# Unit 0 of a gated recurrence with a feed-forward layer: sums of halves as identity matmuls, products unsplit, keys handled by thirds, and one weight tile loaded first

## The chip, the cores and the metric

One NeuronCore of a Trainium2 chip. The metric is device time in microseconds of one execution. Engines are named as in the profile: PE (TensorE matmul; PEld its weight loads), DVE (VectorE), ACT (ScalarE), POOL (GpSimd) and SP (SyncE, which issues most DMAs). Each engine works through its own queue strictly in the order fixed when the program is built; an instruction that has to wait holds up everything behind it on its engine.

## What is computed

```python
mag = sqrt(a_re*a_re + a_im*a_im)
scale = minimum(mag, 0.999) / (mag + 1e-06)          # the decay, kept below 1
a = (a_re + i a_im) * scale                          # per batch, head, time, key channel
for t in range(S):                                   # B, H, S, D = 4, 8, 768, 48
    state = a[t] * state + outer(k[t], v[t])         # complex state, 48 x 48 per head
    y[t]  = q[t] @ real(state)
x   = y, heads side by side                          # 3072 tokens x 384
out = ((x @ w_a) * (x @ w_b)) @ w_out                # d_ff 1536, all float32
```

## The kernel before

The sequence is cut into chunks of 128 steps. A **unit** is a pair of batches in one chunk: 12 units, six chunks for each pair. All eight heads of a unit lie as 384 rows of (head, channel), in three thirds j of 128 partitions, so a quantity of a unit is a tile of 128 partitions x 768 (three thirds x two batches x 128 steps).

A unit passes through these steps.

- `scale(u)` makes the decay factor from the squares of both parts, by Ln and Exp on ACT and one Newton step on DVE. For unit 0 it works in two halves of 384 columns, which load by two DMAs. The sum of the two squares is a DVE operation (L182).
- `prep(u)` multiplies the decays in (L214), then forms running products of them: seven steps within sub-blocks of eight (L230 multiplies, L236 adds; for unit 0 in two parts), a joining of the sub-blocks in small tiles, and then for the real and the imaginary part (k = 0, 1) two 768-wide products (L292) into `a_t` and their sum into `z` (L297). From z it makes the inverse: squares (L300), their sum (L306), Ln and Exp (L307, L308), one Newton step (L322, L324). Queries are multiplied with z (L312); keys with the inverse (L328) and then with z (L312).
- `stack(u)` copies queries and keys head by head into `stk` by ten DMAs from SP; for units 0 and 1 the queries go ahead of the keys.
- `attn(u)` is PE work with DVE and ACT between: scores (L385) and their masking (L388), outputs (L425) into `xh` and `xl`, transposes and the state.
- The feed-forward layer: for each of 12 blocks f of d_ff, `gemm1` (L486) and `gemm2` (L504). Each float32 factor is a pair of fast-format values, hi and lo.

The 36 weight tiles (12 blocks x 3 parts, 128 x 384) come as 64-bit words and are converted on the chip by `split_weights`. For each: three DVE operations (L137, L139, L141) assemble the values in a buffer `o_sb` (a pool of three, taken in turn), ACT rounds them to hi (L145), PE forms the value minus hi in PSUM with an identity and a negated identity (L150, L151), and ACT writes lo (L152). A buffer of o_sb is free again when L145 and L150 have read it. Here 18 tiles are written ahead of attention of unit 0 and 18 are spread over the feed-forward of unit 0, where `prep(1)` runs too. L675 in that stretch is a row of matmuls on the new keys of unit 1 ahead of its attention.

A build-time scheduler (the tile framework) sets the order of each engine's queue from the written order and the dependencies, so the conversions stand between the steps of unit 0, and some of the later 18 tiles too are ahead of its attention. SP issues the loads in the written order: decays of unit 0 in two halves, weight block 0, queries and keys, block 1, values, block 2, decays of unit 1, the other blocks.

Of the kernel before, what the change touches and what calls it, by code (L numbers as in the profile page):

```python
# [8 lines left out]
F32 = mybir.dt.float32  # L9
# [5 lines left out]
ALU = mybir.AluOpType  # L15
# [55 lines left out]
def tile_kernel(ctx: ExitStack, tc: tile.TileContext, a_d, qk_d, v_d, w_d, qn_d, kn_d, vn_d, an_d, out_d):  # L71
# [24 lines left out]
    biases = const.tile([128, 6], F32, name="biases")  # L96
    b_tiny, b_sq, b_eps, b_one, b_inv, b_rsq = (biases[:, i:i + 1] for i in range(6))
    vec.memset(b_tiny, TINY)
    vec.memset(b_sq, EPS * EPS * (1 + 2.0 ** -20))
    vec.memset(b_inv, LIFT * LN2)  # L100
# [24 lines left out]
    def load_weights(f):  # L125
        for m, (c0, n) in enumerate(WPART):
            raws[f, m] = wpool.tile([128, n, 2], U32, name=f"w{m}{f}")
            sync.dma_start(out=raws[f, m].rearrange("p c s -> p (c s)"),
                           in_=w_d[f, :, c0:c0 + n].bitcast(U32))

    def split_weights():
        for f in range(NF):
# [20 lines left out]
            yield  # L153
# [15 lines left out]

    def scale(u, a_t, tmp):  # L170
# [6 lines left out]
        for n, hs in enumerate(halves if u == 0 else (slice(0, W),)):  # L177
# [4 lines left out]
            vec.scalar_tensor_tensor(out=m, in0=m, scalar=-EPS * EPS, in1=x, op0=ALU.add, op1=ALU.add)  # L182
            act.activation(out=s0, in_=m, func=AF.Ln, bias=b_sq)
# [5 lines left out]
            vec.tensor_tensor(out=m, in0=m, in1=x, op=ALU.mult)  # L189
# [13 lines left out]
    def prep(u):  # L203
# [22 lines left out]
        parts = [(p * NB // 2, NB // 2) for p in range(2)] if u == 0 else [(0, NB)]  # L226
        for i in range(1, SUB):
            pr = small.tile([128, 2, 2, NB], F32, name="pr", bufs=1)
            for o, n in parts:
                vec.tensor_tensor(  # L230
                    out=pr[:, :, :, o:o + n],
                    in0=view(zz, W + at_(i) + 2 * o, [[W, 2], [-W, 2], [2, n]]),
                    in1=tok(slice(1, 3), i - 1, o, n).unsqueeze(1).broadcast_to([128, 2, 2, n]),
                    op=ALU.mult)
            for o, n in parts:
                vec.tensor_tensor(out=tok(slice(1, 3), i, o, n), in0=pr[:, :, 0, o:o + n],  # L236
                                  in1=pr[:, :, 1, o:o + n], op=ALU.add)
# [51 lines left out]
        for k in range(2):  # L289
            pz = a_t  # L290
            for s in range(2):
# [5 lines left out]
            vec.tensor_tensor(out=z[:, k].rearrange("p (b i e) -> p b i e", e=2, i=SUB // 2),  # L297
                              in0=view(pz[:], 0, PAIRS), in1=view(pz[:], W, PAIRS), op=ALU.add)
# [7 lines left out]
        vec.tensor_tensor(out=a_t[:, 0], in0=a_t[:, 0], in1=a_t[:, 1], op=ALU.add)  # L306
        act.activation(out=a_t[:, 1], in_=a_t[:, 0], func=AF.Ln, scale=2.0 ** LIFT, bias=b_tiny)  # L307
# [456 lines left out]
```

## Time and profile before

| | |
|---|---|
| median of 3 runs | 698.79 us (698.2 to 699.16) |
| the profiled execution | 698.89 us, span 697.2 us |
| busy: PE, PEld, DVE, ACT, POOL | 655.2, 610.8, 551.8, 308.9, 5.6 us |
| mean TensorE clock of the span | 0.974 of full speed |
| DMA | 63.94 MB, mean 92 GB/s; 300 to 400 GB/s in the first 45 us |

How to read its rows: a row of the timeline is start and duration in us, engine, line, operation, the tile written and those read, partitions x elements, and how many instructions are merged in it (x2); in square brackets stands the engine's idle time before it and what ended that. A float32 matmul shows as two records. Ends of matmuls are modelled. In a row of stretches each engine has its busy us and its number of instructions; then come the granted TensorE clock, the busy share of the DMA engines and GB/s.

### The profile page before, as it was taken

The numbers are of one execution on the slowest core, as the hardware profiler recorded it, in microseconds if no ns is written. First come the engines' busy times: TensorE is split into PE (matmuls) and PEld (weight loads), VectorE is DVE, ScalarE is ACT, GpSimd is POOL, SyncE is SP. The second block draws the span as 40 slices with busy tenths as digits, with TensorE's granted clock in tenths as the row PEclk, the third lists the DMA queues.
The fourth block names the chain that finished last, engine by engine and source line by source line (L and its number), as shares of the span: only waits on it lengthen the run. The fifth ranks groups of instructions, "written<-read, shape, count | busy, mean of one in ns | idle before, by whom it ended". The sixth has DMA issues, their size and how long they took to land.

```text
span 697.2 us, 14316 instructions
## 1 busy us (share of the span) xinstructions
PE 655.2 (94%) x5854; PEld 610.8 (88%) x5854; DVE 551.8 (79%) x1241; ACT 308.9 (44%) x618; POOL 5.6 (1%) x11
## 2 busy tenths in 40 slices
PE   3557999999999999999999999999999999999996
PEld 1224889899899999999999999999999999999996
DVE  5999899988888889989899898999989853232221
ACT  6357755634535445245363554535542332221221
POOL 3000000000000000000000000000000000000000
PEclk9567999999999999999999999999999999999999
DMA  8973202411414205134151340511510500400000
GB/s 312 402 291 108 79 1 54 129 55 55 128 42 130 81 28 149 60 98 129 25 160 46 102 134 1 169 67 47 145 46 2 165 25 17 106 24 2 24 1 28
DMA packets 32088, 63.94 MB, mean 92 GB/s; under 512 B 3984, under 2 KB 10640, under 8 KB 32016
## 3 DMA queue, kind: packets, MB, share of 16 engines
q1 hardware_dynamic: 28560, 58.23, 27.0%
q10 hardware_dynamic: 3456, 4.72, 1.9%
q8 instruction: 48, 0.79, 0.5%
q14 instruction: 24, 0.20, 0.1%
HBM read 39.32 MB, written 4.72 MB: 63 GB/s over the span
## 4 chain that ended last, share of the span: by engine, by line
PE 64%; DVE 27%; ACT 4%; DMA 2%; issue 1%; SPq 1%; ACTq 0%; DVEq 0%
PE ab L486 30%; PE o L504 14%; PE xp L425 6%; PE pm L385 5%; PE pm L442 4%; DVE a_t L292 3%; DVE pr L230 2%; DVE qk L312 2%; DVE h_t L495 2%; PE pm L396 2%; DVE hl L497 2%; PE pm L150 2%; DVE z L297 2%; DVE pb L260 1%; DVE z L236 1%
## 5 line engine op out<-in xcount | busy, mean ns | idle before, releaser
L486 PE MATMUL ab<-xh,w 128*128 128x256 f32 x1728 | 339.0, 285 | 0.0
L486 PEld LDWEIGHTS ab<-xh,w 128*128 128x128 f32 x1728 | 278.1, 190 | 1.8 <-issue 1.4
L486 PE MATMUL ab<-xl,w 128*128 128x256 f32 x864 | 245.1, 284 | 0.0
L486 PEld LDWEIGHTS ab<-xl,w 128*128 128x128 f32 x864 | 164.4, 190 | 0.5 <-issue 0.2
L504 PE MATMUL o<-w,hh 128*128 128x384 f32 x576 | 152.3, 344 | 0.0
L494 ACT COPY h_t<-ab 128x256 f32<-128x256 f32 x144 | 53.1, 369 | 176.9 <-PE ab L486 176.8
L495 DVE TENSOR_TENSOR h_t<-ab,h_t 128x256 f32<-128x256 f32 x144 | 60.5, 420 | 72.5 <-ACT h_t L494 72.3
L504 PEld LDWEIGHTS o<-w,hh 128*128 128x128 f32 x576 | 96.8, 190 | 3.7 <-issue 3.0
L504 PE MATMUL o<-w,hl 128*128 128x384 f32 x288 | 96.9, 336 | 0.0
L496 ACT CAST hh<-h_t 128x256 fp32r<-128x256 f32 x144 | 58.0, 403 | 81.1 <-DVE h_t L495 80.9
L497 DVE TENSOR_TENSOR hl<-h_t,hh 128x256 fp32r<-128x256 f32 x144 | 60.5, 420 | 17.5 <-ACT hh L496 17.3
L150 PE MATMUL ab<-o_sb,ident 128*128 128x384 f32 x42 | 29.1, 794 | 29.9 <-DVE o_sb L141 29.8
L385 PE MATMUL pm<-stk 128*128 128x128 f32 x384 | 54.4, 279 | 2.7 <-DMA stk<-qk 2.7
L504 PEld LDWEIGHTS o<-w,hl 128*128 128x128 f32 x288 | 54.1, 188 | 0.0
L385 PEld LDWEIGHTS pm<-stk 128*128 128x128 f32 x384 | 48.7, 191 | 5.9 <-issue 4.8
L230 DVE TENSOR_TENSOR pr<-z 128x384 f32<-128x384 f32 (+1 forms) x91 | 47.1, 524 | 2.4 <-ACT z L216 0.8
L150 PEld LDWEIGHTS ab<-o_sb,ident 128*128 128x128 f32 x42 | 10.2, 286 | 39.8 <-DVE o_sb L141 29.4
L292 DVE TENSOR_TENSOR a_t<-z,b_t 128x768 f32<-128x768 f32 x48 | 44.6, 952 | 0.1
L425 PE MATMUL xp<-am,v_t 128*32 128x128 f32 x768 | 42.5, 277 | 1.3 <-DVE am L388 1.2
L312 DVE TENSOR_TENSOR qk<-qk,z 128x1536 f32<-128x1536 f32 (+1 forms) x28 | 42.7, 1524 | 0.1
L388 DVE TENSOR_TENSOR am<-pm,mask 128x512 f32<-128x512 f32 x48 | 32.8, 685 | 5.0 <-PE pm L385 4.8
L425 PE MATMUL xp<-stk,u 128*32 128x128 f32 x640 | 34.4, 273 | 0.0
(106 smaller groups left out, 761.7 us busy)
## 6 DMA issues: line engine op xcount, KB each, us to landing
w<-in_dram SPq DMA_DIRECT2D x36, 384.0 KB, 8.1
qk<-in_dram SPq DMA_DIRECT2D x12, 768.0 KB, 4.8
a_t<-in_dram SPq DMA_DIRECT2D x11, 768.0 KB, 4.3
stk<-qk SPq DMA_DIRECT2D x42, 192.0 KB, 3.3
v_t<-in_dram SPq DMA_DIRECT2D x24, 256.0 KB, 2.7
out_dram<-o_sb ACTq DMA_DIRECT2D x24, 192.0 KB, 1.9
stk<-qk SPq DMA_DIRECT2D x18, 192.8 KB, 3.4
stk<-qk SPq DMA_DIRECT2D x14, 128.0 KB, 3.1
```

Of the source, the lines that this page charges most:

```text
L150: pe.matmul(out=lp[:, 0:n], lhsT=ident, rhs=t, start=True, stop=False)
L230: vec.tensor_tensor(out=pr[:, :, :, o:o + n], in0=view(zz, W + at_(i) + 2 * o, [[W, 2], [-W, 2], [2, n]]), in1=tok(slice(1, 3), i - 1, o, ...
L292: vec.tensor_tensor(out=pz[:, s].rearrange("p (j b e) -> p j b e", j=SUB // 2, e=2), in0=zb[:, 1 + s], in1=view(bb, (1 + k - s) * NB, [[0, ...
L312: vec.tensor_tensor(out=qk4[:, :, k, x0:x1], in0=qk4[:, :, 1, x0:x1], in1=z[:, k].rearrange("p (j t) -> p j t", j=NJ).unsqueeze(2).broadca ...
L385: pe.matmul(out=sp[:, h4], lhsT=stk[:, h, ks], rhs=stk[:, h, qs], start=True, stop=True)
L425: pe.matmul(out=xp[qd * 32:(qd + 1) * 32, ti], lhsT=l, rhs=rr, start=st, stop=sp_, tile_position=(0, qd * 32), skip_group_check=True)
L486: pe.matmul(out=ab[:, m * TOK:(m + 1) * TOK], lhsT=r(w_ab(f, part, m * NJ + i)), rhs=r(xt[:, i, :]), start=n == 0, stop=n == 8)
L494: act.copy(out=h_t, in_=ab[:, 0:TOK])
L495: vec.tensor_tensor(out=h_t, in0=ab[:, TOK:2 * TOK], in1=h_t, op=ALU.mult)
L496: act.copy(out=r(hh), in_=h_t)
L497: vec.tensor_tensor(out=r(hl), in0=h_t, in1=hh, op=ALU.subtract)
L504: pe.matmul(out=os_[tt][:, 0:DM], lhsT=r(ht[:, ts]), rhs=r(w_t[f, 2][:, part, :]), start=(f == 0 and n == 0), stop=(f == NF - 1 and n == 2))
```

## The change

All of it concerns unit 0 and what stands around it.

- **Sums on PE.** A function `added` adds two 384-wide tiles as two accumulating identity matmuls into PSUM. It replaces L182 of both halves of `scale(0)`, L297 for both k (ACT then copies the sum from PSUM into z, in the order that z needs), and L306. What followed reads PSUM; EPS*EPS is subtracted where the product is formed.
- **Products unsplit.** The seven steps of the running products are one multiply and one add each, as for the other units.
- **Keys by thirds.** For each third j: the keys times the inverse, times z for both k, and then the DMAs of that third.
- **First weight tile ahead.** Tile 0 of block 0 is loaded before the decays and its conversion is written before `scale(0)`. `split_weights` now yields after each tile rather than after three. The other weights up to block 3 follow the decays; queries and keys, values and the decays of unit 1 come after block 3.

```diff
-    def load_weights(f):
-        for m, (c0, n) in enumerate(WPART):
+    def load_weights(f, ms=range(3)):
+        for m in ms:
+            c0, n = WPART[m]
...
                 act.copy(out=r(lo), in_=lp[:, 0:n])
-            yield
+                yield
...
+    def added(pool, name, x, y):
+        ps = pool.tile([128, 512], F32, name=name)
+        pe.matmul(out=ps[:, 0:W // 2], lhsT=ident, rhs=x, start=True, stop=False)
+        pe.matmul(out=ps[:, 0:W // 2], lhsT=ident, rhs=y, start=False, stop=True)
+        return ps[:, 0:W // 2]
...
-            vec.scalar_tensor_tensor(out=m, in0=m, scalar=-EPS * EPS, in1=x, op0=ALU.add, op1=ALU.add)
-            act.activation(out=s0, in_=m, func=AF.Ln, bias=b_sq)
+            if u == 0:
+                ps = added(ps_m, "pm", t[:, 0], t[:, 1])
+                act.activation(out=s0, in_=ps, func=AF.Ln, bias=b_sq0)
+            else:
...
-            vec.tensor_tensor(out=m, in0=m, in1=x, op=ALU.mult)
+            if u == 0:
+                vec.scalar_tensor_tensor(out=m, in0=ps, scalar=-EPS * EPS, in1=x, op0=ALU.add, op1=ALU.mult)
+            else:
...
-        parts = [(p * NB // 2, NB // 2) for p in range(2)] if u == 0 else [(0, NB)]
         for i in range(1, SUB):
...
+            vec.tensor_tensor(out=pr, in0=view(zz, W + at_(i), [[W, 2], [-W, 2], [2, NB]]),
+                              in1=tok(slice(1, 3), i - 1, 0, NB).unsqueeze(1).broadcast_to([128, 2, 2, NB]),
+                              op=ALU.mult)
+            vec.tensor_tensor(out=tok(slice(1, 3), i, 0, NB), in0=pr[:, :, 0], in1=pr[:, :, 1], op=ALU.add)
...
+            if u == 0:
+                for n, hs in enumerate(halves):
+                    act.copy(out=view(zz, k * W + n * SUB // 2, [[2, SUB // 4], [SUB, NB], [1, 2]]),
+                             in_=added(ps_o, f"o{n}", pz[:, 0, hs], pz[:, 1, hs]))
+            else:
...
+        if u == 0:
+            n2s = [added(ps_m, "pm", a_t[:, 0, hs], a_t[:, 1, hs]) for hs in halves]
+            for n2_, hs in zip(n2s, halves):
+                act.activation(out=a_t[:, 1, hs], in_=n2_, func=AF.Ln, scale=2.0 ** LIFT, bias=b_tiny)
+        else:
...
+        if u == 0:
+            for j in range(NJ):
+                vec.tensor_tensor(out=kk[:, j], in0=kk[:, j], in1=inv[:, j], op=ALU.mult)
+                for k in range(2):
+                    vec.tensor_tensor(out=qk[:, j, k, TOK:2 * TOK], in0=kk[:, j], in1=z[:, k, j * TOK:(j + 1) * TOK],
+                                      op=ALU.mult)
+                stack(u, slice(TOK, 2 * TOK), j)
+            return
...
-    load_weights(0)
-    load_qk(0)
-    load_weights(1)
-    load_v(0)
-    load_weights(2)
-    a_tiles[1] = load_a(1)
-    for f in range(3, NF):
+    load_weights(0, (0,))
     a_first = a_tiles[0] = load_a(0)
+    load_weights(0, (1, 2))
+    for f in range(1, NF):
         load_weights(f)
+        if f == 3:
+            load_qk(0)
+            load_v(0)
+            a_tiles[1] = load_a(1)
...
     ws = split_weights()
+    next(ws)
     drain(scale(0, a_tiles[0], z_first))
     drain(prep(0))
-    stack(0)
     load_qk(1)
     p1 = prep(1)
-    for _ in range(CONV_FIRST):
+    for _ in range(3 * CONV_FIRST - 1):
         next(ws)
```

What this does to the queues is shown at three places. A row is line, operation, tile written and tiles read, and elements; "x2" is two in a row. The numbers behind `w_` count tiles as they are made and differ between the two programs, as do line numbers: L137, L139, L141 before are L139, L141, L143 after; L150, L151 are L152, L153; the two matmuls of `added` are L174 and L175.

The start of PE's queue, before:

```order
L150 MATMUL ab<-o_sb,ident 128x384 x2
L151 MATMUL ab<-w_342,nident 128x384
L150 MATMUL ab<-o_sb,ident 128x384
L151 MATMUL ab<-w_352,nident 128x384
L151 MATMUL ab<-w_362,nident 128x384
```

and after:

```order
L152 MATMUL ab<-o_sb,ident 128x384
L153 MATMUL ab<-w_205,nident 128x384
L174 MATMUL pm<-z,ident 128x384
L175 MATMUL pm<-z,ident 128x384
L174 MATMUL pm<-z,ident 128x384
L175 MATMUL pm<-z,ident 128x384
L152 MATMUL ab<-o_sb,ident 128x384
L153 MATMUL ab<-w_370,nident 128x384
```

The sums of both halves of the decays stand behind the first weight tile and ahead of the second (w_370 is its result).

DVE's queue ahead of the first product of the decays with their factor (L189 before, L202 after), before:

```order
L137 TENSOR_SCALAR o_sb<-w_123 128x384
L139 SCALAR_TENSOR_TENSOR o_sb<-w_123,o_sb 128x384
L137 TENSOR_SCALAR o_sb<-w_125 128x384
L141 SCALAR_TENSOR_TENSOR o_sb<-w_123,o_sb 128x384
L139 SCALAR_TENSOR_TENSOR o_sb<-w_125,o_sb 128x384
L189 TENSOR_TENSOR z<-z 128x384
```

and after:

```order
L139 TENSOR_SCALAR o_sb<-w_128 128x384
L141 SCALAR_TENSOR_TENSOR o_sb<-w_128,o_sb 128x384
L143 SCALAR_TENSOR_TENSOR o_sb<-w_128,o_sb 128x384
L139 TENSOR_SCALAR o_sb<-w_130 128x384
L141 SCALAR_TENSOR_TENSOR o_sb<-w_130,o_sb 128x384
L139 TENSOR_SCALAR o_sb<-w_132 128x384
L143 SCALAR_TENSOR_TENSOR o_sb<-w_130,o_sb 128x384
L202 SCALAR_TENSOR_TENSOR z<-pm,z 128x384
```

w_125 is the third tile; w_128, w_130 and w_132 are the fourth, fifth and sixth. So three more tiles are begun ahead of this product, and in all eight tiles instead of four are converted ahead of the product with the decays (L214 before, L229 after).

DVE's queue around the Newton step of the inverse, before (its first operation is L322):

```order
L306 TENSOR_TENSOR a_t<-a_t 128x768
L141 SCALAR_TENSOR_TENSOR o_sb<-w_154,o_sb 128x384
L137 TENSOR_SCALAR o_sb<-w_156 128x384
L137 TENSOR_SCALAR o_sb<-w_158 128x384
L139 SCALAR_TENSOR_TENSOR o_sb<-w_156,o_sb 128x384
L139 SCALAR_TENSOR_TENSOR o_sb<-w_158,o_sb 128x384
L141 SCALAR_TENSOR_TENSOR o_sb<-w_156,o_sb 128x384
L322 TENSOR_TENSOR a_t<-a_t 128x768
L141 SCALAR_TENSOR_TENSOR o_sb<-w_158,o_sb 128x384
L324 SCALAR_TENSOR_TENSOR a_t<-a_t 128x768
```

and after (L343):

```order
L139 TENSOR_SCALAR o_sb<-w_175 128x384
L141 SCALAR_TENSOR_TENSOR o_sb<-w_175,o_sb 128x384
L143 SCALAR_TENSOR_TENSOR o_sb<-w_175,o_sb 128x384
L343 TENSOR_TENSOR a_t<-pm,a_t 128x384 x2
L347 SCALAR_TENSOR_TENSOR a_t<-a_t 128x768
L354 TENSOR_TENSOR qk<-qk,a_t 128x256 x2
L356 TENSOR_TENSOR qk<-qk,z 128x256 x4
L354 TENSOR_TENSOR qk<-qk,a_t 128x256
L356 TENSOR_TENSOR qk<-qk,z 128x256 x2
```

w_175 is the 24th tile: behind it no conversion is left between the Newton step, the key products and the first mask. Before, seven of these 24 tiles stood behind the last key product.

## What I expect of it, before the run

> **What bounds the kernel now.** I read the page first, then busy time by stretches, then the timeline of the first 80 us, queue by queue. From section 2 of the page, with 17.4 us to a digit:
>
> ```profile
> PE   3557999999999999999999999999999999999996
> DVE  5999899988888889989899898999989853232221
> ```
>
> PE is full from about 75 us to the end; until then DVE is the full one. The stretches (PE, PEld, DVE, ACT, POOL busy, then clock, DMA share, GB/s) say it closer:
>
> ```profile
> 4.65:75.49 70.84, 43.56 (x175) 23.00 (x176) 66.75 (x160) 39.95 (x77) 1.64 (x3) 0.76 0.76 276
> 75.49:122.66 47.17, 47.15 (x323) 42.46 (x321) 45.27 (x112) 29.66 (x64) 0.00 (x0) 1.00 0.13 37
> ```
>
> Up to the first feed-forward matmul (75.49) DVE works 66.75 of 70.84 us, idle 4.1. After it PE is never free and DVE nearly never: idle 1.9 of 47.2. The rows where unit 0's stages begin, and three landings:
>
> ```profile
> 4.65 0.84 ACT L181 ACTIVATE z<-a_t 128x768 f32<-128x768 f32 x1 [2.55 <-DMA a_t<-in_dram]
> 5.82 0.84 ACT L181 ACTIVATE z<-a_t 128x768 f32<-128x768 f32 x1 [0.23 <-DMA a_t<-in_dram]
> 8.47 0.36 DVE L137 TENSOR_SCALAR o_sb<-w 128x384 uint32<-128x384 uint32 x1 [1.12 <-DMA w<-in_dram]
> 8.87 0.56 DVE L139 SCALAR_TENSOR_TENSOR o_sb<-w,o_sb 128x384 uint32<-128x384 uint32 x1
> 9.46 0.56 DVE L141 SCALAR_TENSOR_TENSOR o_sb<-w,o_sb 128x384 uint32<-128x384 uint32 x1
> ...
> 17.95 0.35 DVE L137 TENSOR_SCALAR o_sb<-w 128x384 uint32<-128x384 uint32 x1
> 18.22 1.82 DVE L214 TENSOR_TENSOR z<-a_t,sc 128x768 f32<-128x768 f32 x2
> ...
> 39.09 1.82 DVE L292 TENSOR_TENSOR a_t<-z,b_t 128x768 f32<-128x768 f32 x2
> ...
> 56.25 0.95 DVE L312 TENSOR_TENSOR qk<-qk,z 128x768 f32<-128x768 f32 x1
> ...
> 66.63 0.67 DVE L388 TENSOR_TENSOR am<-pm,mask 128x512 f32<-128x512 f32 x1
> ...
> 69.98 0.69 DVE L388 TENSOR_TENSOR am<-pm,mask 128x512 f32<-128x512 f32 x1 [0.47 <-PE pm L385]
> ```
> ```profile
> 75.49 0.60 PE L486 MATMUL ab<-xh,w 128*128 128x256 f32 x3
> ```
> ```profile
> 3.34 7.64 DMA w<-in_dram
> ```
>
> The first, second, third and fifth transfers landed at 4.65, 5.82, 8.47 and 10.98. And at the end of unit 1's preparation:
>
> ```profile
> 121.71 0.95 DVE L312 TENSOR_TENSOR qk<-qk,z 128x768 f32<-128x768 f32 x1
> ```
> ```profile
> 122.76 3.68 PE L675 MATMUL pm<-qk,ident 128*128 128x256 f32 x16
> ```
>
> PE, never idle, reaches these matmuls 0.1 us after DVE has made their input. So neither has slack here: a delay of either up to this point goes through to the end.
>
> **The work that goes.** In a stream a 768-wide DVE operation takes 0.87 (two 1.82, one 0.95). For the others:
>
> ```profile
> 20.43 0.61 DVE L230 TENSOR_TENSOR pr<-z 128x192 f32<-128x192 f32 x2
> 20.96 0.42 DVE L236 TENSOR_TENSOR z<-pr 128x96 f32<-128x96 f32 x2
> 21.30 0.55 DVE L141 SCALAR_TENSOR_TENSOR o_sb<-w,o_sb 128x384 uint32<-128x384 uint32 x1
> ...
> 82.25 0.55 DVE L230 TENSOR_TENSOR pr<-z 128x384 f32<-128x384 f32 x1
> 82.72 0.42 DVE L497 TENSOR_TENSOR hl<-h_t,hh 128x256 fp32r<-128x256 f32 x1
> 83.06 0.35 DVE L236 TENSOR_TENSOR z<-pr 128x192 f32<-128x192 f32 x1
> 83.33 0.55 DVE L139 SCALAR_TENSOR_TENSOR o_sb<-w,o_sb 128x384 uint32<-128x384 uint32 x1
> ```
>
> So 384 wide is 0.47, 256 wide 0.34, the unsplit add 0.27, L137 0.27 (17.95 to 18.22). DVE loses two L182 adds (0.94) and L297 twice and L306 once (2.61). Unsplitting turns 0.53 + 0.34 into 0.47 + 0.27, seven times: 0.91. The keys by thirds are nine of 0.34 for three of 0.87: 0.45 more. DVE is relieved of 4.0 us. Counted alone, the change is a gain; the waits decide.
>
> **PE's price for a sum.** The same float32 identity matmul stands in the trace at both clocks:
>
> ```profile
> 10.16 0.98 PE L150 MATMUL ab<-o_sb,ident 128*128 128x384 f32 x1 [10.16 <-DVE o_sb L141]
> 10.16 1.62 PE L150 MATMUL ab<-o_sb,ident 128*128 128x384 f32 x2 [10.16 <-DVE o_sb L141]
> 36.58 0.59 PE L150 MATMUL ab<-o_sb,ident 128*128 128x384 f32 x1
> 36.58 0.91 PE L150 MATMUL ab<-o_sb,ident 128*128 128x384 f32 x2
> 52.95 0.81 PE L150 MATMUL ab<-o_sb,ident 128*128 128x384 f32 x2
> 56.38 1.65 PE L150 MATMUL ab<-o_sb,ident 128*128 128x384 f32 x2 [2.45 <-DVE o_sb L141]
> ```
>
> One matmul is two records, each adding 0.64 at half clock and 0.32 at full. A sum of two halves of a tile is four matmuls: 5.1 or 2.6 us, where DVE took 0.94 or 0.87. After an idle stretch of 2.45 us PE is back at half clock.
>
> **Stage 1, to the decays' products** (L214, L229 after). The first weight tile lands at 4.65; DVE converts it in 0.40 + 0.59 + 0.56, to 6.2. The decays are now second and third: 5.82 and 8.47. Transfers four to six I put at 9.7, 11.0 and 12.2, so DVE idles 3.5 us, then converts tiles 2 to 4, 1.46 each, to 14.1. ACT squares the second half to 9.3 and makes the negated identity to 9.7; PE then corrects tile 1 and starts the sums at 10.2. Starting cold, they end by 15.2. Tile 5 needs the buffer of tile 2 (o_sb has three), whose matmul stands behind the sums in PE's queue: free at 16.2, and DVE waits 2.1. From there to L229 stand four tiles and an operation (5.1), eight 384-wide decay operations (3.8) and some 0.7 of waits: 25.8, against 18.22. Four more tiles are done by then (4.8 us). Bounds: 25.0 (third landing at 7.0, the 1.17 spacing of the first two) and 28 (all at half clock, sixth transfer 1.5 later).
>
> **Stage 2, to L292/L301.** Before 20.87 us. Seven more conversion operations of 0.40 stand in it (2.8), unsplitting saves 0.91: 22.8, to 48.6.
>
> **Stage 3, to the last key product.** Before 18.1 (39.09 to 57.20), DVE covering every wait with conversions. The chain there:
>
> ```profile
> 46.29 1.48 ACT L300 ACTIVATE a_t<-z 128x1536 f32<-128x1536 f32 x1 [1.03 <-DVE z L297]
> 47.81 0.96 DVE L306 TENSOR_TENSOR a_t<-a_t 128x768 f32<-128x768 f32 x1
> 48.80 0.94 ACT L307 ACTIVATE a_t<-a_t,biases 128x768 f32<-128x768 f32 x1 [1.02 <-DVE a_t L306]
> 50.05 0.93 ACT L308 ACTIVATE a_t<-a_t,biases 128x768 f32<-128x768 f32 x1
> 51.10 0.95 DVE L322 TENSOR_TENSOR a_t<-a_t 128x768 f32<-128x768 f32 x1
> ```
>
> After, with full clock and the first L301 as zero: k=0 products 1.8, its sums done 3.85; k=1's second product waits for them (same a_t), 3.9 to 4.9; its sums 6.6; two ACT copies 7.5; Square 9.0; squares' sums 11.85; Ln with two casts between 12.6; Exp 13.9. DVE has 11.7 us for this time, so it idles 2.2. Then 0.47 + 0.59 + 0.95 and nine products of 0.34, 5.1 with their start: 19.1. If the first sums run at half clock (PE has nothing just before them), the k=1 sums come 2.3 later: 21.4. I take 20.3, between: 68.9.
>
> By the Trainium skill (TensorE: Matmul & The Clock Gate, Part 1) the clock falls only after an idle window of some 3.4 us, and gaps under 3 us are harmless. By that the sum would use 19.1 and give 704.6. The 56.38 row shows a gap of 2.45 that cost the clock, so I don't rely on it.
>
> **Stage 4, to the first feed-forward matmul.** Before 18.3 us (57.20 to 75.49), with seven tiles of conversion and most of unit 1's decays in it; those tiles are done earlier now. The copies into stk:
>
> ```profile
> 57.22 6.33 SPq L352 DMA_DIRECT2D stk<-qk  x10
> ```
> ```profile
> stk<-qk SPq DMA_DIRECT2D x12, 96.0 KB, 2.3
> ```
>
> Ten issues of 0.63 and 2.3 to land. By thirds the first issue leaves 1.7 before the last product ends, so head 3 lands 3.75 behind it and head 7 6.9. First mask 4.3 behind (9.4 before), second 7.6 (12.8 before), the matmul 5.0 later (5.5 before): 12.6. DVE idles some 5.5 here. Sum: 81.5, against 75.49, so +6.0.
>
> **Stage 5, behind it.** At that point DVE still owes unit 1 two 0.87 products and some 1.4 of scaling, before only two conversion operations (0.94): 2.2 late. Of this its 1.9 us of idle time in the next 47 us can take some: 0.3 to 2.2, I take 0.9. Later units are unchanged. Shift +6.9; the profiled run took 698.89 (0.1 over the median of 698.79): 705.8.
>
> **Rivals.** All follow from one balance: shift = DVE idle after − 4.1 idle before − 4.0 relief, so DVE may idle 8.1 us before the change loses. My walk has about 15.
> - Faster: the sums cost DVE no wait. PE is at full clock from the first sum on, tile 2's buffer is free in time and k=1 is covered by conversions; with the third landing at 7.0 only 2.0 at the start and 4.3 at the copies are left, 6.3 in all: −1.8, 697.1. For it: DVE's relief and the earlier copies are real. Against: three rows at half clock, and the queue orders.
> - Much slower: half clock in both groups of sums and landings as late as 28 allows: 28 + 22.8 + 22.4 + 13.5 = 86.7, +11.2, nothing of the 2.2 taken up: 712.3. For it: the 56.38 row.
> - No change: half of the 15 falls away (an early landing saves 1.5, full clock 2.0, shorter waits at the copies 3.5): 8, 698.9. For it only that each of my terms could be high.
>
> **Chances.** Forecast (702 to 709) 0.67, faster 0.14, much slower 0.10, no change (within 0.2%, about what a measurement tells) 0.09. So faster 0.14, same 0.09, slower 0.77. The low end of the range is the faster rival's time, 697, the high end stops short of the full price of the slow one, 711.5.
>
> **What would show it.** Right: the first conversion near 4.7, L229 near 26, the first L301 near 49, DVE gaps at 6 to 10 and 14 to 16 and ahead of L343, the first L519 matmul near 81, and from there the same spacing as before. Wrong: DVE busy throughout and L519 before 75; L174 records of 0.6 from the start; or a first unit that takes the delay up, with L519 late and the end not.

## The result, and the profile after

The changed kernel takes 709.51 us (median of 4 runs, 709.12 to 710.01) against 698.5 for the kernel before on the same chip: ratio 1.0158, 95% interval 1.014 to 1.0175. It is 11 us slower, where 6.9 were forecast: inside the range of 697 to 711.5, but above the 702 to 709 that had the chance of 0.67, and a little nearer to the 712.3 of "much slower" than to the 705.8 of the sum. The profiled execution's span is 707.8 us, +10.6 over the 697.2 of before.

The same two lines of the page's section 2, with 17.7 us to a digit:

```profile
PE   5765999999999999999999999999999999999996
DVE  5997599988988898889989899998999973233221
```

The fourth and the fifth digit (53 to 88 us) are the new thing: DVE at 7 and 5 there, where it had 9 and 8. The stretch up to the first feed-forward matmul says how much (PE, PEld, DVE, ACT, POOL busy, clock, DMA share, GB/s):

```profile
3.90:82.14 78.24, 53.97 (x207) 29.61 (x208) 63.54 (x147) 42.76 (x83) 2.48 (x3) 0.83 0.66 241
```

DVE idles 78.24 − 63.54 = 14.7 us in it; I had put that at about 15. The timeline of DVE shows where; the bracket is its idle time before a row and what ended it:

```profile
3.96 1.55 DVE L139 TENSOR_SCALAR o_sb<-w 128x384 uint32<-128x384 uint32 x1 [2.79 <-DMA w<-in_dram]
...
8.51 0.36 DVE L139 TENSOR_SCALAR o_sb<-w 128x384 uint32<-128x384 uint32 x1 [1.81 <-DMA w<-in_dram]
...
14.33 0.36 DVE L139 TENSOR_SCALAR o_sb<-w 128x384 uint32<-128x384 uint32 x1 [1.36 <-PE ab L152]
...
24.69 1.82 DVE L229 TENSOR_TENSOR z<-a_t,sc 128x768 f32<-128x768 f32 x2
...
47.49 1.81 DVE L301 TENSOR_TENSOR a_t<-z,b_t 128x768 f32<-128x768 f32 x2
...
61.26 1.02 DVE L343 TENSOR_TENSOR a_t<-pm,a_t 128x384 f32<-128x384 f32 x2 [1.35 <-ACT a_t L327]
...
65.78 0.88 DVE L356 TENSOR_TENSOR qk<-qk,z 128x256 f32<-128x256 f32 x2
...
71.00 0.69 DVE L421 TENSOR_TENSOR am<-pm,mask 128x512 f32<-128x512 f32 x1 [2.60 <-PE pm L418]
...
76.19 0.69 DVE L421 TENSOR_TENSOR am<-pm,mask 128x512 f32<-128x512 f32 x1 [4.49 <-PE pm L418]
```

And PE's rows for the three groups of sums and for unit 0's scores:

```profile
9.15 1.48 PE L174 MATMUL pm<-z,ident 128*128 128x384 f32 x2
...
12.78 0.81 PE L175 MATMUL pm<-z,ident 128*128 128x384 f32 x2
...
48.49 1.56 PE L174 MATMUL o<-a_t,ident 128*128 128x384 f32 x4 [1.62 <-DVE a_t L301]
...
56.50 0.91 PE L174 MATMUL pm<-a_t,ident 128*128 128x384 f32 x2
...
67.53 1.24 PE L418 MATMUL pm<-stk 128*128 128x128 f32 x4 [8.01 <-DMA stk<-qk]
...
74.92 2.50 PE L418 MATMUL pm<-stk 128*128 128x128 f32 x10
...
82.14 0.60 PE L519 MATMUL ab<-xh,w 128*128 128x256 f32 x3
```

The decays' sums ran at half speed up to about 12: the first records stand 0.64 us apart, those from 12.78 on 0.32. (The profile's clock figure reads 1.00 for these first us, there and in the kernel before, so that this rests on the spacing.) The sums of z and of the squares ran at full clock. Ahead of the scores PE waits 8.0 us, until a copy into stk has landed, and then ten score matmuls take 2.50 us. Before, with conversions in that stretch, they took 1.38:

```profile
69.23 1.38 PE L385 MATMUL pm<-stk 128*128 128x128 f32 x10
```

Two-us stretches of the changed kernel (third figure from the end is the granted clock) show the half clock there:

```profile
60.00:62.00 2.00, 0.00 (x0) 0.00 (x0) 0.74 (x2) 1.63 (x4) 0.00 (x0) 1.00 0.45 115
62.00:64.00 2.00, 0.00 (x0) 0.00 (x0) 1.93 (x5) 0.00 (x0) 0.00 (x0) 0.94 0.50 131
64.00:66.00 2.00, 0.00 (x0) 0.00 (x0) 1.97 (x7) 0.16 (x1) 0.00 (x0) 0.50 0.00 1
...
74.00:76.00 2.00, 2.00 (x11) 1.39 (x11) 0.00 (x0) 0.00 (x0) 0.00 (x0) 0.50 0.37 98
76.00:78.00 2.00, 2.00 (x25) 1.72 (x24) 1.71 (x3) 0.00 (x0) 0.00 (x0) 0.64 0.77 295
78.00:80.00 2.00, 2.00 (x30) 1.68 (x26) 1.76 (x4) 1.64 (x3) 0.00 (x0) 1.00 0.00 0
```

Up to the first feed-forward matmul the loss is 82.14 − 75.49 = 6.65. The other 4 us arise later, though PE's idle time there grows by 1.4 us only (10.0 before, 11.4 after; the lines stand below, under "The later units"). Roughly where they arise can be read from the rows of one instruction that stands once in every block of every unit, the subtraction that makes `hl` (L497 before, L530 after). First of unit 3 (block 36 counted from the start), then block 54, in unit 4, then block 138, near the end. The kernel before:

```profile
257.89 0.42 DVE L497 TENSOR_TENSOR hl<-h_t,hh 128x256 fp32r<-128x256 f32 x1
...
326.96 0.41 DVE L497 TENSOR_TENSOR hl<-h_t,hh 128x256 fp32r<-128x256 f32 x1
...
673.08 0.42 DVE L497 TENSOR_TENSOR hl<-h_t,hh 128x256 fp32r<-128x256 f32 x1 [0.47 <-ACT hh L496]
```

The changed kernel:

```profile
264.65 0.41 DVE L530 TENSOR_TENSOR hl<-h_t,hh 128x256 fp32r<-128x256 f32 x1
...
337.72 0.41 DVE L530 TENSOR_TENSOR hl<-h_t,hh 128x256 fp32r<-128x256 f32 x1
```

So the delay is +6.76 at block 36, near the +6.9 that I forecast for the end, and +10.76 at block 54; at block 138 it is +10.03. A single block is a rough mark, though: `hl` itself stands elsewhere in the new order, and its delay wanders between 4.8 and 11.2 us from block to block before it is flat at 10.0 from block 114 on.

### The profile page after: what moved, and what is told of

Its sections match the earlier page's. It is cut to its first block, busy times and chain, and to the rows that moved or that the text cites. A ratio compares the mean times of both kernels' runs of the same rounds, so it can differ in the third digit from the quotient of the medians.

```text
span 707.8 us, 14384 instructions
## 1 busy us (share of the span) xinstructions
PE 668.2 (94%) x5886; PEld 618.0 (87%) x5886; DVE 550.4 (78%) x1230; ACT 312.1 (44%) x623; POOL 5.7 (1%) x11
## 4 chain that ended last, share of the span: by engine, by line
PE 62%; DVE 25%; DMA 6%; ACT 3%; issue 1%; SPq 1%; ACTq 0%; DVEq 0%
PE ab L519 28%; PE o L537 14%; PE xp L458 6%; PE pm L418 6%; PE pm L475 4%; DVE a_t L301 3%; DMA w<-in_dram 2%; DVE qk L331 2%; PE pm L429 2%; DMA stk<-qk 2%; DVE hl L530 2%; DVE h_t L528 2%; DMA a_t<-in_dram 2%; DVE pb L269 1%; DVE pr L243 1%
## 5 line engine op out<-in xcount | busy, mean ns | idle before, releaser
L530 DVE TENSOR_TENSOR hl<-h_t,hh 128x256 fp32r<-128x256 f32 x144 | 60.5, 420 | 14.8 <-ACT hh L529 14.6
L418 PE MATMUL pm<-stk 128*128 128x128 f32 x384 | 58.9, 292 | 11.3 <-DMA stk<-qk 11.2
L418 PEld LDWEIGHTS pm<-stk 128*128 128x128 f32 x384 | 51.0, 199 | 16.2 <-issue 13.8
L243 DVE TENSOR_TENSOR pr<-z 128x384 f32<-128x384 f32 x84 | 46.7, 556 | 3.7 <-ACT z L231 2.0
L301 DVE TENSOR_TENSOR a_t<-z,b_t 128x768 f32<-128x768 f32 x48 | 45.3, 952 | 0.1
L458 PE MATMUL xp<-am,v_t 128*32 128x128 f32 x768 | 44.5, 280 | 0.5 <-DVE am L421 0.5
L331 DVE TENSOR_TENSOR qk<-qk,z 128x1536 f32<-128x1536 f32 (+1 forms) x26 | 40.7, 1567 | 0.2
L152 PE MATMUL ab<-o_sb,ident 128*128 128x384 f32 x42 | 23.2, 641 | 17.6 <-DVE o_sb L143 15.3
L475 PEld LDWEIGHTS pm<-v_t,kt 128*96 128x96 f32 x320 | 31.6, 164 | 2.6 <-issue 1.8
```

The lines of the kernel that those rows point to most:

```text
L243: vec.tensor_tensor(out=pr, in0=view(zz, W + at_(i), [[W, 2], [-W, 2], [2, NB]]), in1=tok(slice(1, 3), i - 1, 0, NB).unsqueeze(1).broadcas ...
L301: vec.tensor_tensor(out=pz[:, s].rearrange("p (j b e) -> p j b e", j=SUB // 2, e=2), in0=zb[:, 1 + s], in1=view(bb, (1 + k - s) * NB, [[0, ...
L331: vec.tensor_tensor(out=qk4[:, :, k, x0:x1], in0=qk4[:, :, 1, x0:x1], in1=z[:, k].rearrange("p (j t) -> p j t", j=NJ).unsqueeze(2).broadca ...
L418: pe.matmul(out=sp[:, h4], lhsT=stk[:, h, ks], rhs=stk[:, h, qs], start=True, stop=True)
L458: pe.matmul(out=xp[qd * 32:(qd + 1) * 32, ti], lhsT=l, rhs=rr, start=st, stop=sp_, tile_position=(0, qd * 32), skip_group_check=True)
L475: pe.matmul(out=kp[0:KS, h4 * D:(h4 + 1) * D], lhsT=kts[i, hg][:, h4, :], rhs=v_t[:, o:o + D], start=True, stop=True)
```

## The experiments

Twelve kernels were run. All differ from the kernel before or from the changed kernel by the edit shown; to those made from the kernel before, one memset of a column and the generator that yields after each tile come along. The marks below come from one profiled execution of each: the first product with the decays (L229), the first product of z (L301), the end of the last key product, the first feed-forward matmul, and the delay of `hl` against before at blocks 36 and 138. Line numbers are those of the changed kernel. The time is the median; beside these twelve the kernel before stood at 698.6 to 698.9. In three kernels the profiled execution was well off the median, and the marks carry that: thirds alone (profiled at 700.96), no z sums (714.66) and no decays' sums (705.99).

| kernel | time | ratio to before, 95% | L229 | L301 | keys end | first f.-f. | block 36 | block 138 |
|---|---|---|---|---|---|---|---|---|
| before | 698.8 | | 18.22 | 39.09 | 57.20 | 75.49 | 0 | 0 |
| changed | 709.51 | 1.0158 (1.014 to 1.0175) | 24.69 | 47.49 | 66.66 | 82.14 | +6.76 | +10.03 |
| sums alone | 705.99 | 1.0104 (1.0087 to 1.0121) | 23.68 | 44.56 | 64.44 | 81.18 | +5.55 | +5.68 |
| tile alone | 698.95 | 1.0002 (0.9992 to 1.0012) | 19.83 | 40.72 | 58.54 | 75.04 | −0.47 | −0.48 |
| unsplit alone | 697.93 | 0.9988 (0.9978 to 0.9997) | 17.57 | 40.83 | 58.63 | 75.03 | −0.93 | −0.93 |
| thirds alone | 699.70 | 1.0014 (1.0004 to 1.0024) | 18.33 | 39.20 | 57.70 | 76.84 | +2.19 | +2.18 |
| changed, no sums | 700.65 | 1.002 (1.0006 to 1.0035) | 19.11 | 41.91 | 60.21 | 77.76 | +1.13 | +1.34 |
| changed, no z sums | 712.42 | 1.0193 (1.0176 to 1.021) | 24.79 | 47.71 | 70.30 | 86.29 | +10.74 | +15.48 |
| changed, no decays' sums | 707.23 | 1.0127 (1.0108 to 1.0146) | 18.80 | 41.58 | 63.03 | 77.59 | +2.25 | +6.96 |
| changed, no thirds | 707.56 | 1.0126 (1.0109 to 1.0143) | 25.08 | 48.34 | 67.12 | 84.60 | +8.98 | +9.01 |
| changed, no early tile | 709.86 | 1.0157 (1.014 to 1.0174) | 24.20 | 47.45 | 67.11 | 83.28 | +7.79 | +11.05 |
| changed, filler on PE | 707.66 | 1.0129 (1.0112 to 1.0146) | 24.95 | 47.76 | 66.94 | 83.42 | +8.42 | +8.41 |
| changed, 24 tiles ahead | 702.90 | 1.0057 (1.004 to 1.0074) | 24.50 | 47.77 | 68.27 | 82.92 | +1.94 | +3.84 |
| changed, nine matmuls | 707.11 | 1.0121 (1.0102 to 1.014) | 25.13 | 47.93 | 67.12 | 82.52 | +7.69 | +7.73 |

### Each part alone

First the kernel before with one part of the change each. The first weight tile and the order of the loads:

```diff
     # kernel before, and only:
+    load_weights(0, (0,))
     a_first = a_tiles[0] = load_a(0)
-    load_weights(0)
-    load_qk(0)
-    load_weights(1)
-    load_v(0)
+    load_weights(0, (1, 2))
...                    # blocks 1 to 3, then load_qk(0), load_v(0), load_a(1)
+    next(ws)
     drain(scale(0, a_tiles[0], z_first))
```

> The kernel before with the first weight tile loaded and converted ahead of the decays, and the later load order, alone. Theory A: within 2 us of before: DVE starts 4.5 us earlier and the decays land some 1.7 us later. Rival B (the load order is the loss): 5 to 10 us slower, the first product of decays and factor 4 us or more later with fewer than two more tiles converted ahead of it.

Measured: 698.95, no difference, theory A. Its L229 is 1.6 later and its first feed-forward matmul 0.45 earlier: what is converted early only changes places with what follows.

The three groups of sums:

```diff
     # kernel before, and only:
+                ps = added(ps_m, "pm", t[:, 0], t[:, 1])
...
+                    act.copy(..., in_=added(ps_o, f"o{n}", pz[:, 0, hs], pz[:, 1, hs]))
...
+            n2s = [added(ps_m, "pm", a_t[:, 0, hs], a_t[:, 1, hs]) for hs in halves]
```

> The kernel before with the sums on PE alone (all three groups; products split, keys whole, loads and first weight tile as before). Theory A (the sums make DVE wait, and pull conversions ahead of the waits that they used to cover): 3 to 9 us slower than before, DVE idle 8 to 13 us between its first conversion and the first feed-forward matmul, against 4. Rival B (the load order delays the decays): within 2 us of before. Rival C (DVE's relief of 3.5 us reaches the end and the loss is elsewhere): 2 to 4 us faster.

Measured: 705.99, +7.1, theory A; DVE idles 10.7 us of the 73.8 between its first conversion and the first feed-forward matmul. So the sums by themselves cost 7.1 of the 11 us.

The products unsplit:

```diff
     # kernel before, and only:
-        parts = [(p * NB // 2, NB // 2) for p in range(2)] if u == 0 else [(0, NB)]
+            vec.tensor_tensor(out=tok(slice(1, 3), i, 0, NB), in0=pr[:, :, 0], in1=pr[:, :, 1], op=ALU.add)
```

> The kernel before with the seven product steps unsplit, alone. Theory A: DVE is relieved of 0.9 us and the end comes 0 to 1.5 us earlier. A rival by which a longer dependent step stalls DVE: 1 to 3 us later, with idle time of DVE ahead of the adds.

Measured: 697.93, −0.9, as the forecast's 0.91 for this edit. Its delay is flat at about −0.9 from unit 3 on, and it is the one version here that beats both kernels, by an interval just clear of no change.

The keys by thirds:

```diff
     # kernel before, and only:
+            for j in range(NJ):
+                vec.tensor_tensor(out=kk[:, j], in0=kk[:, j], in1=inv[:, j], op=ALU.mult)
...
+                stack(u, slice(TOK, 2 * TOK), j)
...
-    stack(0)
```

> The kernel before with keys multiplied and copied to stk by thirds, alone. Theory A: the first copy of keys leaves some 1.7 us earlier relative to the last product, DVE gets 0.45 us more: 0 to 2 us faster than before, since DVE has conversions to do in this stretch anyway and PE starts its scores only behind its own conversion matmuls. Rival (copies are the bound of this stretch): 3 to 5 us faster.

Measured: 699.70, +0.8. Theory A and its rival both forecast a gain, and neither came. The first copy of keys does leave earlier against the last product, yet nothing is won. Here is its DVE at the first two masks:

```profile
67.97 0.69 DVE L427 TENSOR_TENSOR am<-pm,mask 128x512 f32<-128x512 f32 x1 [0.60 <-PE pm L424]
...
71.33 0.69 DVE L427 TENSOR_TENSOR am<-pm,mask 128x512 f32<-128x512 f32 x1 [0.47 <-PE pm L424]
```

The first mask stands 10.3 us behind the last key product, where before it was 9.4, and DVE has waited only 0.60 and 0.47 for the scores. I read from this that the conversions that fill the stretch set the masks' time there, and not the copies; no run tested it by itself.

Together the four give +7.1: −0.9, +0.1, +0.8, +7.1. The change made +11. What the other 4 are was open.

### One part taken out of the change

The change without any of its sums on PE:

```diff
-            if u == 0:
+            if False:        # at all three groups
                 ps = added(ps_m, "pm", t[:, 0], t[:, 1])
```

> The change without its sums on PE: DVE adds the decays' squares, the products of z and the squares of the inverse as before; the first weight tile, the unsplit products and the keys by thirds are kept. Theory A (each sum on PE makes DVE wait, and these waits are all of the loss, with the other parts only placing conversions ahead of them): the sums' price is what the change costs in all, 698.9 +- 1.5, some 10 to 12 below the changed kernel, with DVE idle at most 8 us ahead of the first feed-forward matmul and that matmul at 74 to 77. Theory B (the parts cost what each cost alone, and the 4 us between their sum of +7.0 and the measured +11.0 come from the tile and the thirds emptying the stretch around the copies): the three without the sums would still hold that 4: 702 to 704.

Measured: 700.65 (its runs spread from 697.4 to 702.2). That lies between the two theories, nearer to A: A's time ended at 700.4 and its first feed-forward matmul at 77 (77.76 here), while DVE's idle time, 6.8 us, is within its 8; B began at 702. Without the sums some 9 of the 11 us are gone. Only some 5.6 of them are gone by block 36 (+1.13 against +6.76), and this kernel also has another order of its later units, so that the 9 is not the price of the sums alone.

The change without the sums of z on PE:

```diff
-            if u == 0:
+            if False:
                 for n, hs in enumerate(halves):
                     act.copy(..., in_=added(ps_o, f"o{n}", pz[:, 0, hs], pz[:, 1, hs]))
```

> The change, but the two sums of the products of z are made on DVE again (two operations of 768, 1.74 us more work for DVE); the decays' sums and the squares' sums stay on PE. Theory A (waits on PE's sums are the loss, by length of each): the z sums hold back the squares by about 8 us of PE and ACT (eight matmuls and two copies) against 2.7 us of DVE and the wait of the second product; 3 to 4 us are saved, 705.5 to 706.5, with the last key product some 4 earlier. Theory B (the wait at the copies takes up what is saved, since conversions are all done by then anyway): 709 +- 1.

Measured: 712.42, three slower than the change. Both theories missed. Its first squares' sum on PE and DVE's wait behind:

```profile
56.24 1.65 PE L174 MATMUL pm<-a_t,ident 128*128 128x384 f32 x2 [5.11 <-ACT a_t L314]
```
```profile
62.72 0.36 DVE L139 TENSOR_SCALAR o_sb<-w 128x384 uint32<-128x384 uint32 x1 [3.90 <-ACT a_t L323]
```

With the z sums, in the changed kernel, PE came to the squares' sums at full clock (0.91 for two records at 56.50). Without them it has waited 5.1 us and does them at half clock (1.65), and DVE, which has run out of work that it could do, waits 3.9. So the z sums, the largest of the three groups, keep PE busy, and with it the clock up, for the next ones. From L301 to the last key product this kernel takes 22.6 us, the changed one 19.2.

The change without the decays' sums on PE:

```diff
-            if u == 0:
+            if False:
                 ps = added(ps_m, "pm", t[:, 0], t[:, 1])
```

> The change, but the decays' squares are added on DVE again (two operations of 384); the sums of z and of the squares stay on PE. Theory A (the decays' sums cost the start: L229 came 6.5 us later than before with them, 0.9 later without any sums): L229 at 19 to 20 instead of 24.7, and because fewer tiles are then done early, the later waits find cover: 702 to 704. Theory B (what the start wins is idled away at the copies, where 24 tiles is all that can be converted ahead): the first feed-forward matmul some 3 earlier only, 706 to 707.5.

Measured: 707.23 (705.99 to 708.41). By time that is theory B, by the marks theory A: L229 at 18.80, the first feed-forward matmul at 77.59 (4.55 earlier than in the change), +2.25 at block 36. The decays' sums thus make 4.5 us of unit 0's loss. Then the delay grows to +6.96, and that growth is no part of either theory.

The change without the thirds, and without the early tile:

```diff
-        if u == 0:
+        if False:
             for j in range(NJ):
                 vec.tensor_tensor(out=kk[:, j], in0=kk[:, j], in1=inv[:, j], op=ALU.mult)
...
     drain(prep(0))
+    stack(0)
```

> The change, but the keys of unit 0 are multiplied 768 wide and copied after the queries, as before. Alone the thirds cost +0.8. Theory A (in the changed kernel no conversion is left for the wait at the copies, so an earlier first key copy is worth the whole of what it is early, and PE, waiting shorter, is less cold): without the thirds the wait ahead of the scores grows by 1 to 3 us and the time is 710 to 713. Theory B (the thirds cost here what they cost alone, or more, since they leave PE cold in the same way): 707 to 709.

```diff
-    load_weights(0, (0,))
     a_first = a_tiles[0] = load_a(0)
-    load_weights(0, (1, 2))
+    load_weights(0)
+    load_qk(0)
+    load_weights(1)
+    load_v(0)
...
-    next(ws)
```

> The change, but the loads are in the order of before and no conversion stands ahead of the decays. Alone this part cost nothing (+0.15). Theory A (the early tile and the early weights pull conversions ahead of the waits, so that nothing is left to fill them): without it two tiles fewer are converted ahead of the decays' products and the DVE waits at the start (4.1 us) shrink to some 2: 707 to 708.5. Theory B (the number of tiles ahead of the products doesn't matter, as all 24 are done by the key products in either): 709.5 +- 0.7.

Measured: 707.56 and 709.86. Both agree with theory B by time. But without the thirds the first feed-forward matmul comes 2.5 us later than in the change and the end 2 us earlier, so again something behind unit 0 weighs more than what is in it.

### The wait at the copies

Five identity matmuls ahead of unit 0's scores:

```diff
+    wp = ps_m.tile([128, 512], F32, name="pm")
+    for i in range(5):
+        pe.matmul(out=wp[:, 0:TOK], lhsT=ident, rhs=inv_of[0][:, 0, 0:TOK], start=True, stop=True)
     x_cur = new_x()
```

(`inv_of[0]` is the tile `a_t` of unit 0, whose first half is the inverse of the keys.)

> The changed kernel with five identity matmuls of 256 on PE behind the inverse of the keys and ahead of unit 0's scores, whose results nothing reads; all else as it was. In the changed kernel PE idles 8.0 us there, the granted clock falls to 0.50 at about 64 and is back at 1.00 only at 78, and the scores and outputs between run at half speed. Theory A (that half clock is the part of the forecast's stage 4 that was missed, 15.5 us against 12.6): the five matmuls run from 63.2 to 67.8, the clock is back near 68 instead of 77, ten scores matmuls take 1.4 instead of 2.5, the second mask comes 2 to 3 us earlier, the first feed-forward matmul at 79.3 to 80.3, and the time is 706.5 to 707.8. Theory B (the scores wait for the copies whatever the clock, and conversions owed set what follows): the clock is back, the end is not: 709.5 +- 0.7.

Measured: 707.66, in theory A's bounds, but not by theory A. The rows of PE and DVE:

```profile
63.60 4.11 PE L668 MATMUL pm<-a_t,ident 128*128 128x256 f32 x10 [3.81 <-DVE a_t L348]
...
69.44 0.46 PE L420 MATMUL pm<-stk 128*128 128x128 f32 x2 [0.70 <-DMA stk<-qk]
...
74.72 2.50 PE L420 MATMUL pm<-stk 128*128 128x128 f32 x10
```
```profile
75.98 0.69 DVE L423 TENSOR_TENSOR am<-pm,mask 128x512 f32<-128x512 f32 x1 [4.32 <-PE pm L420]
```

and its stretches:

```profile
66.00:68.00 2.00, 1.91 (x7) 1.08 (x5) 0.87 (x3) 0.20 (x1) 0.00 (x0) 0.61 0.39 103
68.00:70.00 2.00, 1.18 (x6) 0.66 (x5) 0.59 (x1) 1.38 (x2) 0.00 (x0) 1.00 0.41 105
70.00:72.00 2.00, 1.26 (x4) 0.80 (x4) 1.06 (x2) 1.57 (x2) 0.00 (x0) 0.74 0.43 106
72.00:74.00 2.00, 1.86 (x12) 1.20 (x12) 0.00 (x0) 1.94 (x3) 0.00 (x0) 0.50 0.29 79
```

The clock came back, for some 3.4 us by these shares, and fell again near 71, while the scores wait for one copy after the other and PE is busy only 59 and 63% of 68 to 72. The ten score matmuls take 2.50 us as in the changed kernel, the second mask is 0.2 earlier, the first feed-forward matmul 1.3 later. Nothing is won in unit 0; the 2 us are won behind it. So what unit 0 would take with a clock that stays up in this stretch is not shown by this run.

Six more tiles written ahead of unit 0's attention, 24 instead of 18 (`CONV_ON_AB` lets their sums use the PSUM buffers `ab` too):

```diff
-CONV_ON_AB = 7
+CONV_ON_AB = 9
-CONV_FIRST = 6
+CONV_FIRST = 8
```

> The changed kernel, but 24 weight tiles instead of 18 are written ahead of unit 0's attention (and the first 27 instead of 21 use the PSUM buffers ab), so that 28 tiles stand ahead of the first mask in DVE's queue and 30 ahead of unit 1's first decays' product, where there were 24 for both. DVE's work up to the end of unit 1's preparation is the same. Theory A (the loss is DVE idle time, and the 7.1 us idle at the scores are idle because 24 tiles is all that could be converted by then): the four to six tiles fill some 4 to 6 us of it, they are not owed later, their matmuls keep PE working so that it is not at half clock, and the matmuls on unit 1's keys come 4 to 7 us earlier: 702.5 to 705.5. Theory B (the delay is the chain sums, inverse, keys, copies, scores, which sets the feed-forward's start whatever DVE does meanwhile): 708 to 710, with the first feed-forward matmul at 82 and the same spacing behind it.

Measured: 702.90, theory A. The waits of 2.60 and 4.49 at the masks have become:

```profile
72.86 0.69 DVE L421 TENSOR_TENSOR am<-pm,mask 128x512 f32<-128x512 f32 x1 [1.31 <-PE pm L418]
...
76.19 0.69 DVE L421 TENSOR_TENSOR am<-pm,mask 128x512 f32<-128x512 f32 x1 [0.84 <-PE pm L418]
```

The second mask stands where it stood and the first feed-forward matmul is 0.8 later, yet the end is 6.6 us earlier. The matmuls on unit 1's keys come 2.1 us earlier (129.96 against 132.05), not the 4 to 7 that theory A had. The stretch up to the first feed-forward matmul:

```profile
3.91:82.92 79.01, 60.88 (x238) 33.54 (x238) 70.71 (x165) 47.53 (x97) 2.48 (x3) 0.85 0.65 240
```

DVE idles 8.3 us in it, where it idled 14.7. In the changed kernel that time was idle because the next conversions were not to be had: DVE's queue has no more than 24 tiles ahead of the masks, and here it has begun 29 by the first mask. PE did later work in this stretch too: six tiles' matmuls, some 0.8 us of PE a tile in a row of them, no longer stand in the feed-forward, where PE is full. So idle time that was filled is a gain, but whether DVE's or PE's counts was not separated. This kernel also has an order of its own in the later units, which can hold up to 3 of the 6.6 us (next section); against the kernel with nine matmuls there, which has the order of before, it is 4.2 us faster.

### The later units

Which kernels lose more behind the first feed-forward matmul? By the table, from that matmul to block 138, the delay grows by 3.4 us in the changed kernel, and by 4.7, 4.9 and 3.3 in those without z sums, without decays' sums and without the early tile; in all of the others by at most 0.8. Most of it shows between blocks 36 and 54: 4.0, 5.5, 5.4 and 4.0. The order of PE's matmul records in the traces tells the kernels apart (a float32 matmul is two records, and a trace has 5854 to 5896). The four that grow share the last 5792, all that stands behind unit 0's sums. The tile, the products and the thirds alone and the kernel with the filler share the last 4649 or more with the kernel before. The sums alone, the change without sums and that without thirds have a third order: they share the last 5202 with each other but only 2539 with the kernel before, and from the first feed-forward matmul to block 138 their delay changes by 0.0, −0.9 and −0.1. So not every new order costs; that of the four does. (The kernel with 24 tiles ahead has yet another, up to the last 3920.) To test that the order does it, the changed kernel got a ninth matmul in the row of eight on unit 1's keys. Up to there its queues are those of the changed kernel, and behind it nearly all of PE's queue, the last 4635 records of the trace, is that of before:

```diff
-WARM = 8
+WARM = 9
```

> The changed kernel with nine instead of eight identity matmuls of 256 on unit 1's keys (0.46 us more for PE, read by nothing). Up to them the queues of all engines are those of the changed kernel, word for word. Behind them the scheduler's order differs: the last 4409 instructions of PE's queue are those of the kernel before, where the changed kernel has an order of its own in which only the last 1761 agree. Theory A (some 3 us of the loss are not in unit 0 at all: in the changed kernel and in the three variants that share its later order the delay grows by 3 to 5 us between 276 and 330 us, in the others by 0.6 or less, except the one with 24 tiles ahead, which grows by 1.9; so the order of units 1 to 8 costs it): the first feed-forward matmul at 82 as in the changed kernel, the delay flat at +6.5 to +8 from unit 3 on, 705.5 to 707.3. Theory B (the later delay is unit 0's, given back late by DVE, whatever the order): 709.5 to 710.5, growing at 276 to 330 us as in the changed kernel.

Measured: 707.11, theory A. Its rows at blocks 36, 54 and near the end:

```profile
265.58 0.42 DVE L530 TENSOR_TENSOR hl<-h_t,hh 128x256 fp32r<-128x256 f32 x1
...
334.69 0.42 DVE L530 TENSOR_TENSOR hl<-h_t,hh 128x256 fp32r<-128x256 f32 x1
```

+7.69 and +7.73, flat to the end. And the stretch between these two blocks in the kernel before, the changed kernel and this one, in this order:

```profile
257.89:326.96 69.07, 68.98 (x637) 67.64 (x636) 63.73 (x129) 36.43 (x69) 0.00 (x0) 1.00 0.38 111
```
```profile
264.65:337.72 73.07, 72.90 (x667) 70.10 (x668) 63.49 (x130) 37.96 (x70) 0.00 (x0) 1.00 0.34 100
```
```profile
265.58:334.69 69.11, 69.01 (x637) 67.67 (x636) 63.67 (x129) 36.47 (x69) 0.00 (x0) 1.00 0.38 111
```

With the order of before the stretch is that of before, to the record. In the changed kernel it lasts 4.0 us longer at full clock, but it also holds 30 matmul records more, so that part of the four us is work that only stands elsewhere in the order. The whole rest of the program, from the first feed-forward matmul to the end, has no such doubt. Again the kernel before, the changed one and the one with nine matmuls:

```profile
75.49:697.20 621.71, 611.69 (x5682) 587.82 (x5680) 484.82 (x1074) 267.64 (x541) 0.00 (x0) 1.00 0.24 70
```
```profile
82.14:707.80 625.66, 614.24 (x5682) 588.43 (x5680) 486.53 (x1075) 268.10 (x540) 0.00 (x0) 1.00 0.24 71
```
```profile
82.52:705.20 622.68, 612.01 (x5684) 588.19 (x5682) 485.79 (x1075) 267.50 (x540) 0.00 (x0) 1.00 0.24 71
```

The same number of matmul records takes 4.0 us longer in the changed kernel than before, 2.6 of them as busy time of PE and 1.4 as idle time. With the ninth matmul, two records more, most of that is gone. One matmul of 0.46 us more made the kernel 2.4 us faster (2.6 in the profiled spans); the order of the later units is therefore worth some 3. Which wait or which mix of matmuls loses the time inside PE's busy stretch was not settled.

## Why the forecast was right and where it was wrong

The direction and the reason were right: DVE is relieved of its adds and waits longer than that for what PE makes in their place. By the steps:

- **Stage 1** (L229 at 25.8, measured 24.69). Right in its mechanism, 1.1 high by terms that partly cancel. Too high were the landing of tile 2 (converted from 8.51, not 9.7), the start of the sums (9.15, not 10.2) and the wait for tile 2's buffer (1.36, not 2.1, as the last sum ran at full speed). Too low was the way from there to L229, 10.4 us instead of 9.6.
- **Stage 2** (22.8). Measured 22.80, with the seven conversion operations and the unsplit products.
- **Stage 3** (20.3, between 19.1 at full clock and 21.4). Measured 19.2. The k = 0 sums took 1.56 for four records after an idle time of 1.62: full clock. The rule of the Trainium skill that I set aside (TensorE: Matmul & The Clock Gate, Part 1), by which the clock falls after an idle window of some 3.4 us, would have given the right figure, 19.1, and for this wait of 1.62 us the trace agrees with it. It is no rule for every place, though: with the filler matmuls the clock came back and then fell to 0.50 with no gap over 0.70 us in between.
- **Stage 4** (12.6). Measured 15.5. The first mask came 4.3 behind the last product as forecast, the second 9.5 instead of 7.6, the first matmul 6.0 behind it instead of 5.0. The term that was mis-sized is PE's: I let it work at full clock after a wait of 8.0 us, though I had the row of 56.38 in hand. Between the masks PE is all but never idle and its clock is 0.50. Where the ten score matmuls took 1.38 us again, with 24 tiles ahead, the second mask came 7.9 behind the last product, close to the 7.6. That the filler did not buy this back does not contradict it, since the filler did not hold the clock either; so the half clock is read from the rows, and no run removed it alone.
- **The sum of unit 0**: first feed-forward matmul at 82.14, forecast 81.5. Two errors of −1.1 and one of +2.9 nearly cancel: that the sum came so close is luck, though the waits in it are the right ones. DVE's idle time, 14.7, was forecast as about 15.
- **Stage 5** (+0.9). With the nine matmuls, from the first feed-forward matmul (+7.03) to the end (+7.73), 0.7 is added, of which 0.46 is the ninth matmul. That leaves 0.2, just under the low end of 0.3 to 2.2 and 0.7 less than the sum used. Unit 0's own loss is some 7.3 where 6.9 was forecast, again with two errors that nearly cancel.
- **"Later units are unchanged"** is the sentence that failed. Their code is unchanged, their order is not: the scheduler places all instructions of the program in one run, and with the change it placed units 1 to 8 otherwise. That cost some 3 of the 11 us, and the forecast put it at nothing. The order of the queues can be read from the built program ahead of the run; the forecast used it only where unit 0 stands.

Of the rivals, "faster" fails by its conditions: the clock was half at the first sums, the buffer of tile 2 was late, and DVE idled 14.7 us where 8.1 was the limit. "Much slower" came nearest to the time, by the wrong road: it had half clock in both groups of sums, where only the decays' had it, and L229 at 28, where it stands at 24.69. "No change" fails with them: DVE's idle time was not halved.

The parts alone (+7.1) and the change with the order of before (707.11, less 0.46, so some 7.8 over before) leave hardly any interaction in unit 0: the four us that seemed to come of putting the parts together were for some three of the four the order.

## What to carry to other kernels

Where an engine is full, moving an operation off it gains only what it can do instead while it waits; count its idle time after the move and look for work that can still be pulled into it, as six more tiles did here. An engine that takes over small work in a sparse stretch may do it at half clock, as the decays' sums show, and the work that it had there before may be what kept the clock up, as the z sums show. And compare the whole order of the built program, not only the part that was edited: an order of later units that no line of the change touches was worth some 3 us, and a single matmul more turned it.

## What the runs showed of the hardware that I had not expected

- The clock fell after different idle times. In the changed kernel it fell some 4 us after PE's last matmul (which ended near 59.5; 0.94 over 62 to 64, then 0.50); in the kernel before, 2.4 us after one (which ended near 53.9; 1.00 over 54 to 56, 0.57 over 56 to 58). In the filler kernel it had taken some 4 us of busy PE to rise (63.6 to 67.6), and it fell some 3.4 us later, with PE 59 to 63% busy. Yet in the changed kernel the clock stayed up for 10 us with PE 44 to 67% busy, on wider matmuls. The first and the last of these five stretches:

```profile
38.00:40.00 2.00, 1.15 (x5) 0.48 (x3) 2.00 (x7) 0.99 (x2) 0.00 (x0) 1.00 1.04 404
...
46.00:48.00 2.00, 0.87 (x4) 0.27 (x2) 2.00 (x8) 0.96 (x3) 0.00 (x0) 1.00 0.10 37
```

  So neither the longest gap nor the busy share by itself, as the profile counts it, tells when the clock falls; what does was not found.
- The first conversion operation, started as soon as its tile had landed at 3.96, took 1.55 us where the others take 0.36; it took 1.43 to 1.55 in the nine kernels that load a weight tile first, and 0.36 in those that load it after the decays. In all nine it starts between 3.96 and 4.10 and ends at 5.51 to 5.53, 0.2 us behind a long operation of POOL that is over when the others start:

```profile
1.78 3.52 POOL L111 MEMSET stk<- 32x4112 f32 x1
```

  By this it was POOL's memset that held it; no run moved the memset.
